# Letting the loads of batches 4 to 7 go one tile sooner

## The chip, the cores and the metric

The kernel runs on one core of a Trainium2 chip. The metric is the device time of one execution in microseconds (us). A profile covers one further execution, and its span (from the first to the last instruction) is about 1.8 us shorter than the time of the same execution.

Engines: PE is the tensor engine, DVE the vector engine, ACT the scalar engine, POOL is GpSimd and SP is SyncE. SP and POOL issue almost all DMAs here. "SPq" and "POOLq" are their queues.

## The reference, cut to what matters

```python
# q, k, v: (8 batches, 8 heads, 576 positions, 64)
kv  = np.einsum('bhsd,bhse->bhde', k, v)
out = np.einsum('bhsd,bhde->bhse', q, kv)
rms = np.sqrt(np.mean(out * out, axis=-1, keepdims=True) + 1e-06)
x   = (out / rms * g_norm)          # then reordered to (8, 576, 512)
xn  = (x - mean(x)) / np.sqrt(var(x) + 1e-06) * g_ln
y   = x + np.maximum(xn @ w_ch1, 0.0) @ w_ch2     # 512 -> 2048 -> 512
```

The 8 x 576 rows make 36 tiles of 128 rows, and four tiles make a block: blocks 0 to 8. Block 5 is tiles 20 to 23.

## The kernel before: the parts that matter

Before it emits anything, the kernel runs a small scheduler over all its steps, with guessed costs. That plan fixes the order of the instructions on each engine. What the chip then does is wait for semaphores in that order.

For batches 3 to 7, k and q are loaded by POOL straight into the layout in which they are used; q is then transposed by one large DMA on SP's queue (`q_turn_dma`, giving qT). Each tile's normalised rows xc are transposed by a smaller DMA on the same SP queue (`t_turn_dma`, giving xT). The first matmul of a block (L598) needs the xT of all its four tiles.

```python
def t_turn_dma(n):                                   # L544
    m, i = divmod(n, 4)
    nc.sync.dma_start_transpose(
        blk[m]["xT"][:, :, i * 128:(i + 1) * 128], st[n]["xc"])

def q_turn_dma(b):                                   # L421
    att[b]["qT"] = work.tile([128, 20, 128], bf16, tag="qT", name="qT", bufs=3)
    nc.sync.dma_start_transpose(
        att[b]["qT"], qp[b % 2].rearrange("p t h d -> p (t h d)"))
```

The loads don't go as soon as their buffer is free. POOL first runs a "gate": a copy of a single element out of the xT of an earlier tile, so that POOL, which runs in order, waits until that transpose has landed. With f the first tile of batch b (18, 22, 27 and 31 for batches 4 to 7), k, q and v wait for tiles f-7, f-6 and f-5:

```python
f = FIRST[b]
def gate(n):
    if b >= 3:
        m, i = divmod(n, 4)
        pool_do(0.1, lambda: nc.gpsimd.tensor_copy(                       # L691
            mark, blk[m]["xT"][:, 0, i * 128:i * 128 + 1]), done[n]["xT"])
# ...
gate(f - 7 if b > 3 else 5)
gate_turn()                                          # L695: waits for the last batch's qT
# ... load k
def some_q():
    gate(f - 6 if b > 3 else 6)
    # ... load q
def some_v():
    gate(f - 5 if b > 3 else 7)
    # ... load v
# ...
turn = add_dma("SP", ok - 12, qperm + load["q", b] + ..., lambda: q_turn_dma(b), ...)
turn.lag = 5.0 if by_slot else 0.0                   # for the plan alone
```

## Time and profile before

| | kernel before |
|---|---|
| time, first three runs | 296.15 us median (296.14 to 296.57) |
| span of the profiled execution | 295.1 us |
| PE busy | 283.1 us |
| PE idle before an instruction, before 26 us | 2.3 + 4.3 + 0.7 + 0.4 us |
| PE idle before an instruction, after 26 us | 0.7 us, once |

The busy time of PE, from the first part of the page:

```profile
span 295.1 us, 5184 instructions
PE 283.1 (96%) x2061; PEld 161.1 (55%) x2061; DVE 165.8 (56%) x360; ACT 143.1 (49%) x288; POOL 66.0 (22%) x92
```

The waits of PE (who waited, for whom, us in total, how often, the longest):

```profile
PE kv_ps L429 <- DMA vb<-in_v_dram: 4.3, 1, 4.3
PE scale_ps L308 <- DMA scales<-in_moe_g_ln_dram: 2.3, 1, 2.3
PE mm_ps L598 <- DMA xT<-xc: 0.7, 1, 0.7
PE mm_ps L583 <- ACT xT L540: 0.7, 1, 0.7
PE mm_ps L583 <- DMA w<-in_moe_w_ch_dram: 0.4, 1, 0.4
```

Four of these five waits come before 26 us, during the first loads. The third line is the only one later on. The timeline of PE around it (start, length, what; in brackets the idle time before it) shows that it is the start of block 5:

```profile
173.13 2.11 PE L617 MATMUL mm_ps<-w,m 128*128 128x512 bf16 x9
175.94 0.81 PE L598 MATMUL mm_ps<-xT,w 128*128 128x512 bf16 x3 [0.69 <-DMA xT<-xc]
```

What led to it stands in the timeline of the two issuing engines, from 153 us on. L261 is the load of q of batch 6, L233 the load of its v, L421 its qT, L544 an xT:

```profile
154.68 2.01 POOL L261 DMA_DIRECT2D qp<-in_q_dram  x1 [0.43 <-issue]
156.56 1.19 SPq L544 DMA_TRANSPOSE xT<-xc  x1
164.06 0.19 POOL L691 COPY mark<-xT 128x1 bf16<-128x1 bf16 x1 [6.68 <-DMA xT<-xc]
164.26 3.16 SPq L421 DMA_TRANSPOSE qT<-qp  x1
164.66 0.89 POOL L233 DMA_DIRECT2D vb<-in_v_dram  x1 [0.42 <-issue]
...
167.51 1.68 SPq L544 DMA_TRANSPOSE xT<-xc  x1
```

The transpose of tile 22 went at 156.56. The next in the queue was qT of batch 6, which had to wait for q; it went at 164.26. Tile 23, whose xc DVE had finished at 163.63, went at 167.51. The same instruction, looked at alone (its transfer, issue to landing):

```profile
L544 SPq DMA_TRANSPOSE xT<-xc x1: 1683/1683/1683, 167.5 to 167.5; - x1
...
DMA to landing us min/median/max: 8.1/8.1/8.1
```

So tile 23 stood 3.9 us in the queue and then flew 8.15 us, while the median xT flies 3.7 us. It landed at 175.66.

### The profile page before, as it was taken

To read this page: it belongs to the slowest core of one execution; us is meant where nothing else is said; L and a number is where in the kernel's file an instruction comes from. 1 tells how busy PE (TensorE), PEld (TensorE's weight loads), DVE (VectorE), ACT (ScalarE), POOL (GpSimd) and SP (SyncE) were. 2 spreads that over 40 slices of the span, in tenths; PEclk is the share of its full clock that TensorE was granted. 3 is DMA by queue.
4 is the path that set the end of the run, shared out by engine and by line. 5 is a ranking of instruction groups with operands and counts; after the bars stand their busy time and mean duration, and the time that the engine had idled before them with its cause. 6 is when DMAs were issued, how large, how long until landed. Compare 5 with 4: busy or idle time off the path is not lost.

```text
span 295.1 us, 5184 instructions
## 1 busy us (share of the span) xinstructions
PE 283.1 (96%) x2061; PEld 161.1 (55%) x2061; DVE 165.8 (56%) x360; ACT 143.1 (49%) x288; POOL 66.0 (22%) x92
## 2 busy tenths in 40 slices
PE   3799999999999999999999999999999999999995
PEld 1789955877745445444544445544454444444444
DVE  1397038759876886557655773577557755420022
ACT  3178972986857612671267117621762177006500
POOL 8882230208207024320403207020000000000000
PEclk9999999999999999999999999999999999999999
DMA  6999999749999998998399799999201310210012
GB/s 91 176 196 206 203 199 192 181 89 106 188 176 82 139 120 200 161 120 168 93 131 86 107 185 130 137 134 178 56 18 53 91 53 18 56 71 35 0 73 72
DMA packets 107388, 35.21 MB, mean 119 GB/s; under 512 B 85603, under 2 KB 103395, under 8 KB 107364
## 3 DMA queue, kind: packets, MB, share of 16 engines
q0 software_dynamic: 72608, 18.35, 65.2%
q1 hardware_dynamic: 34516, 16.39, 23.5%
q8 instruction: 16, 0.26, 0.4%
q10 hardware_dynamic: 240, 0.13, 0.2%
q14 instruction: 8, 0.07, 0.1%
HBM read 36.70 MB, written 9.44 MB: 156 GB/s over the span
## 4 chain that ended last, share of the span: by engine, by line
PE 87%; DMA 10%; POOL 1%; issue 1%; DVE 1%; ACT 0%; ACTq 0%; POOLq 0%
PE mm_ps L617 39%; PE mm_ps L598 33%; PE mm_ps L583 8%; DMA w<-in_moe_w_ch_dram 4%; DMA xT<-xc 3%; PE kv_ps L429 3%; PE out_ps L452 3%; DMA kb<-in_k_dram 3%; PE xT_ps L533 1%; PE qT_ps L401 0%; POOL qp L254 0%; POOL kb L233 0%; POOL w L334 0%; DVE ss L474 0%; POOL vb L233 0%
## 5 line engine op out<-in xcount | busy, mean ns | idle before, releaser
L617 PE MATMUL mm_ps<-w,m 128*128 128x512 bf16 (+2 forms) x608 | 130.3, 368 | 0.0
L598 PE MATMUL mm_ps<-xT,w 128*128 128x512 bf16 x448 | 100.8, 379 | 0.7 <-DMA xT<-xc 0.7
L605 ACT ACTIVATE m<-mm_ps 128x512 bf16<-128x512 f32 x112 | 66.8, 597 | 51.2 <-PE mm_ps L598 50.2
L617 PEld LDWEIGHTS <-m 128*128 128x128 bf16 x608 | 57.0, 98 | 59.7
L598 PEld LDWEIGHTS <-w 128*128 128x128 bf16 x448 | 43.0, 98 | 49.5 <-issue 1.2
L624 DVE SCALAR_TENSOR_TENSOR x<-mm_ps,rstd,x 128x512 f32<-128x512 f32 (+2 forms) x38 | 27.3, 721 | 41.9 <-PE mm_ps L617 41.8
L474 DVE TENSOR_REDUCE ss<-sq 128x8 f32<-128x512 f32 (+1 forms) x37 | 24.8, 670 | 46.0 <-ACT sq L465 45.9
L465 ACT ACTIVATE sq<-out_ps 128x512 f32<-128x512 f32 (+1 forms) x37 | 21.5, 584 | 52.3 <-PE out_ps L452 52.3
L583 PE MATMUL mm_ps<-xT,w 128*128 128x128 bf16 x512 | 30.9, 219 | 1.0 <-ACT xT L540 0.7
L583 PEld LDWEIGHTS <-w 128*128 128x128 bf16 x512 | 29.3, 98 | 2.1 <-issue 0.8
L526 DVE SCALAR_TENSOR_TENSOR xc<-x,mv,gl 128x512 bf16<-128x512 f32 (+1 forms) x37 | 27.1, 737 | 1.4 <-DVE mv L521 0.3
L469 DVE TENSOR_TENSOR xg<-out_ps,gn 128x512 f32<-128x512 f32 (+1 forms) x37 | 24.8, 669 | 0.3
L691 POOL COPY mark<-xT 128x1 bf16<-128x1 bf16 x15 | 5.1, 340 | 80.4 <-DMA xT<-xc 67.8
L590 ACT ACTIVATE m<-mm_ps 128x512 bf16<-128x512 f32 x32 | 18.3, 597 | 3.2 <-PE mm_ps L583 2.5
L504 DVE TENSOR_TENSOR x<-xg,inv 128x512 f32<-128x512 f32 x24 | 16.6, 693 | 0.8
L520 DVE BATCH_NORM_STATS2 stats<-x 128x6 f32<-128x512 f32 x24 | 16.6, 690 | 0.5
L444 DVE CAST kv_pack<-kv_ps 64x256 bf16<-64x256 f32 (+1 forms) x18 | 7.1, 392 | 15.8 <-PE kv_ps L429 15.7
L478 ACT ACTIVATE rms<-ss,eps_attn 128x8 f32<-128x8 f32 (+1 forms) x37 | 11.0, 298 | 9.9 <-DVE ss L474 9.9
L429 PE MATMUL kv_ps<-vb,kp 128*128 128x128 bf16 (+1 forms) x144 | 11.5, 231 | 4.3 <-DMA vb<-in_v_dram 4.3
L452 PEld LDWEIGHTS <-qT 128*128 128x128 bf16 x160 | 11.6, 98 | 7.3 <-DVE kv_pack L444 0.3
L452 PE MATMUL out_ps<-kv_pack,qT 128*128 128x128 bf16 x160 | 14.9, 220 | 0.1
L429 PEld LDWEIGHTS <-kp 128*128 128x128 bf16 (+1 forms) x168 | 10.9, 103 | 5.6 <-issue 2.6
(61 smaller groups left out, 171.4 us busy)
## 6 DMA issues: line engine op xcount, KB each, us to landing
out_dram<-x SPq DMA_DIRECT2D x28, 256.0 KB, 2.8
w<-in_moe_w_ch_dram POOLq DMA_DIRECT2D x8, 512.0 KB, 12.5
vb<-in_v_dram POOLq DMA_DIRECT2D x6, 512.0 KB, 9.1
kp<-in_k_dram POOLq DMA_DIRECT2D x5, 512.0 KB, 8.2
qp<-in_q_dram POOLq DMA_DIRECT2D x5, 512.0 KB, 9.5
out_dram<-x SPq DMA_DIRECT2D x14, 128.0 KB, 2.5
qb<-in_q_dram POOLq DMA_DIRECT2D x2, 512.0 KB, 15.7
qp<-in_q_dram POOLq DMA_DIRECT2D x10, 64.0 KB, 8.4
```

Source lines behind the costliest of these rows:

```text
L429: nc.tensor.matmul(ps[:, hp, :], lhsT=kp[b % 2][p, t, 2 * hp:2 * hp + 2, :].rearrange("p h d -> p (h d)"), rhs=(v5[b % 2][:, 2 * hp:2 * hp ...
L452: nc.tensor.matmul(o3[:, hp, :], lhsT=att[b]["qT"][:, 4 * t + hp, :], rhs=kv_pack[b % 3][:, hp, :], start=(i == 0), stop=(i == len(bs) - 1))
L465: nc.scalar.activation(sq[:, h0:h1, :], st[n]["ps", h0][:, h0:h1, :], func=AF.Square)
L469: nc.vector.tensor_mul(xg[:, h0:h1, :], st[n]["ps", h0][:, h0:h1, :], gn.to_broadcast([128, h1 - h0, D]))
L474: nc.vector.tensor_reduce(ss[:, h0:h1, :], st[n]["sq"][:, h0:h1, :], axis=AX.X, op=ALU.add)
L526: nc.vector.scalar_tensor_tensor(xc[:, f0:f1], in0=st[n]["x"][:, f0:f1], scalar=blk[m]["mv"][:, i, 0:1], in1=gl[:, f0:f1], op0=ALU.subtrac ...
L583: nc.tensor.matmul(ps[:, d, :], lhsT=w1[c][:, kk, d * 128:(d + 1) * 128], rhs=blk[m]["xT"][:, kk, i * 128:(i + 1) * 128], start=(kk == 0), ...
L590: nc.scalar.activation(st[n]["m1"][:, c, :, :], st[n]["m1ps", c], func=AF.Relu)
L598: nc.tensor.matmul(ps, lhsT=w1[c][:, kk, d * 128:(d + 1) * 128], rhs=blk[m]["xT"][:, kk, :], start=(kk == 0), stop=(kk == nKm - 1))
L605: nc.scalar.activation(blk[m]["m1", c][:, d, :], blk[m]["m1ps", g], func=AF.Relu)
L617: nc.tensor.matmul(st[n]["m2ps", f0], lhsT=m1_piece(n, c, d), rhs=w2[c][:, d, f0:f1], start=(c == 0 and d == 0), stop=(c == 3 and d == 3))
L624: nc.vector.scalar_tensor_tensor(x[:, f0:f1], in0=st[n]["m2ps", f0], scalar=blk[m]["rstd"][:, i, :], in1=x[:, f0:f1], op0=ALU.mult, op1=AL ...
```

## The change

The intent is to let each of these loads go one tile sooner, so that it lands earlier and what waits for it has more room.

```diff
-            gate(f - 7 if b > 3 else 5)
+            gate(f - 8 if b > 3 else 5)
             gate_turn()
@@ some_q @@
-                gate(f - 6 if b > 3 else 6)
+                gate(f - 7 if b > 3 else 6)
@@ some_v @@
-                gate(f - 5 if b > 3 else 7)
+                gate(f - 6 if b > 3 else 7)
```

The number of instructions doesn't change (the traces below count 5184 and 5183; now and then a record is missing from a trace). On PE, DVE, ACT and POOL their order is the same as before. On SP, the plan moves qT of batch 6 ahead of tile 22, and qT of batch 7 ahead of tile 26.

## The prediction

> **What bounds the kernel.** The tensor engine. The page gives PE 283.1 of 295.1 us busy, granted clock 1.00 throughout. Summing the idle times before PE instructions in the list of waits: 2.3 + 4.3 + 0.7 + 0.4 us, all before 26 us, during the first loads; after that one wait is left, of 0.7 us at 175.9 us, on L598 (first matmul of block 5, tiles 20 to 23), for the DMA transpose xT<-xc of tile 23. The change touches nothing before 85 us, so 0.7 us (0.24% of the time) is all that it can win; it could lose more.
>
> **What it does.** It adds and removes no instruction. The twelve one-element copies on GpSimd that hold back the loads of k, q and v for batches 4 to 7 wait for the transposed tile before the one they waited for. The instruction orders: PE, DVE, ACT and POOL the same; on SP the qT transposes of batches 6 and 7 move ahead of one xT transpose (tiles 22 and 26).
>
> **Where loads can move**, from the timeline (issue; landing):
> - Batch 4: k is held until the previous qT lands (89.15), so k (89.95) and q (92.43) stay; v goes from 103.4 to about 95.5.
> - Batch 5: k (114.7) and q (117.6) stay, held by qT at 113.93; v goes from 127.1 to about 120.
> - Batch 6: k 144.5 to about 140; q 154.7 to about 149.5; v 164.7 to about 158.
> - Batch 7: k 179 to about 169; q 181.4 to about 178; v 193 to about 185.
>
> **The one wait.** xc of tile 23 was ready at 163.63, but the SP queue stood at the qT transpose of batch 6, which waited for q (landed 163.92 and 164.11). So tile 23 was issued at 167.51, and landed at 175.66, 8.1 us later against a median of 3.7, beside that qT transpose (landed 174.99) and v (174.63). The Trainium skill, "DMA: Bandwidth & Descriptors", section "Issuing engines are not separate DMA queues", says that DMAs of all issuers run on the same 16 engines and interleave; the trace agrees: xT takes 2.4 us alone, 8.1 us beside both. After the change q of batch 6 lands at about 159, qT is issued then, tile 23 at about 163.7, landing at 167 to 171, before PE wants it at 175.2. The wait goes.
>
> **What it costs.** k, q and v follow each other more closely, so xT transposes of tiles 13, 14, 17, 21, 22 and 25 share the engines more and land up to about 6 us later; tiles 22 and 26 also stand behind qT in the queue (22: about 156.6 to 162; 26: 187 to 191). What counts is the last tile of each block: tile 15 had 4.9 us to spare (landed 110.96, wanted 115.8), tile 19 6.1 us, tile 27 2.9 us (202.84 against 205.8). I expect 15 and 19 to keep over 2 us and tile 27 to gain, as v and qT of batch 7 are earlier. DVE and ACT are half idle and don't set the pace.
>
> **Time.** 296.15 - 0.7 = 295.5 us; range 295.1 to 296.3. Faster by over 2%: 0.005; within 2%: 0.985; slower by over 2%: 0.01.
>
> **What would show it.** Right: span about 294.4; no PE wait after 30 us; tile 23 issued near 163.7; v of batch 4 issued near 95.5; PE busy time unchanged. Wrong: a PE wait at 115.8, 145.4, 175.2 or 205 us on xT; or tile 23 still behind qT because q of batch 6 landed no earlier.
>
> **What would make it wrong.** Crowded loads delaying tile 15, 19, 23 or 27 by more than its slack: each us beyond it costs one us. Or run-to-run scatter of the first loads (296.14 to 296.57 before), as large as the effect.

## The result, and the profile after

Ratios are computed as the mean time of one kernel's fast runs over the mean time of the other's fast runs of the same rounds, so they are not quite the ratio of the medians quoted.

| | before | after |
|---|---|---|
| time, six runs each | 296.16 us median (294.80 to 296.57) | 295.35 us median (295.18 to 295.76) |
| ratio | | 0.998, 95% interval 0.9959 to 1.0 |
| span of the profiled execution | 295.06 us | 293.96 us |
| start of block 2 | 85.72 | 85.33 |
| block 4 start to block 5 start | 30.49 | 29.64 |
| tile 23: xc ready, issued, landed | 163.63, 167.51, 175.66 | 163.24, 163.67, 166.17 |
| block 5 starts | 175.94 | 174.69 |

The page and the waits of PE after:

```profile
span 294.0 us, 5183 instructions
PE 283.4 (96%) x2061; PEld 161.6 (55%) x2061; DVE 166.1 (57%) x360; ACT 143.3 (49%) x288; POOL 65.5 (22%) x92
```

```profile
PE kv_ps L429 <- DMA vb<-in_v_dram: 3.1, 1, 3.1
PE scale_ps L308 <- DMA scales<-in_moe_g_ln_dram: 2.2, 1, 2.2
PE qT_ps L401 <- DMA qp<-in_q_dram: 0.8, 1, 0.8
PE mm_ps L583 <- ACT xT L540: 0.7, 1, 0.7
```

The wait on xT is gone, and the other waits are still those of the first 26 us. The timeline of PE at the start of block 5 (no idle time in brackets any more), of the issuing engines before it, and tile 23 alone:

```profile
174.69 2.11 PE L598 MATMUL mm_ps<-xT,w 128*128 128x512 bf16 x9
```

```profile
147.79 2.01 POOL L261 DMA_DIRECT2D qp<-in_q_dram  x1 [0.42 <-issue]
...
154.39 0.89 POOL L233 DMA_DIRECT2D vb<-in_v_dram  x1
...
156.30 5.07 SPq L421 DMA_TRANSPOSE qT<-qp  x1
161.46 3.43 SPq L544 DMA_TRANSPOSE xT<-xc  x2
```

```profile
L544 SPq DMA_TRANSPOSE xT<-xc x1: 1219/1219/1219, 163.7 to 163.7; - x1
...
DMA to landing us min/median/max: 2.5/2.5/2.5
```

q of batch 6 is issued 6.9 us sooner and v 10.3 us sooner. qT goes at 156.30, ahead of tile 22. Tile 23 is issued 0.43 us after its xc is ready and flies 2.5 us, because v had landed at 160.56 and the next load (k of batch 7) went only at 167.19. It lands 8.5 us before PE asks for it.

Where did the 1.10 us of span go? All but one of the stretches between the starts of blocks 2 to 8 are the same to 0.01 us in both traces. Block 4 to block 5 gives 0.85 us. The start of block 2 gives 0.39 us, before any changed load is issued. The stretch from the start of block 8 to the end is 0.15 us longer after (31.48 against 31.33), for which no cause was looked for. The 0.69 us of idle time on PE thus stands for 0.85 us of time: the stretch is the better measure of what this wait costs, since the idle time is taken from modelled ends of matmuls.

### The profile page after: what moved, and what is told of

The parts are those of the page before. It is cut to its first block, busy times and chain, and to the rows that moved or that the text cites. A ratio compares the mean times of both kernels' runs of the same rounds, so it can differ in the third digit from the quotient of the medians.

```text
span 294.0 us, 5183 instructions
## 1 busy us (share of the span) xinstructions
PE 283.4 (96%) x2061; PEld 161.6 (55%) x2061; DVE 166.1 (57%) x360; ACT 143.3 (49%) x288; POOL 65.5 (22%) x92
## 2 busy tenths in 40 slices
DMA packets 107388, 35.21 MB, mean 120 GB/s; under 512 B 85603, under 2 KB 103395, under 8 KB 107364
## 4 chain that ended last, share of the span: by engine, by line
PE 90%; DMA 7%; POOL 1%; issue 1%; DVE 0%; POOLq 0%
PE mm_ps L617 42%; PE mm_ps L598 33%; PE mm_ps L583 8%; DMA w<-in_moe_w_ch_dram 5%; PE kv_ps L429 3%; PE out_ps L452 3%; DMA vb<-in_v_dram 3%; PE xT_ps L533 1%; POOL kb L233 1%; PE qT_ps L401 0%; POOL vb L233 0%; DVE x L624 0%; POOL qp L254 0%; POOLq L943 0%
## 5 line engine op out<-in xcount | busy, mean ns | idle before, releaser
L691 POOL COPY mark<-xT 128x1 bf16<-128x1 bf16 x15 | 6.3, 423 | 64.2 <-DMA xT<-xc 55.4
```

## The experiments

**Theories.** The main theory was that of the prediction: the gain is the one wait for tile 23, and it goes because q of batch 6 lands sooner, so that tile 23 doesn't stand behind qT. Rivals: (A) the loads of every batch have a share; (B) the difference is scatter of the first loads; (C) the changed order on SP gives the gain, not the earlier loads; (D) and (E) only the sharing of the DMA engines, or only the standing in the queue, matters.

The first four ran together on one chip, beside 11 runs of the kernel before (295.58 us median, 294.99 to 297.0).

### Batch 6 alone

```diff
-gate(f - 7 if b > 3 else 5)
+gate(f - (8 if b == 6 else 7) if b > 3 else 5)
```

and the same for q and v.

> Only batch 6's three loads are let go one tile sooner; batches 4, 5 and 7 as before. Main theory (the gain is the one PE wait of 0.7 us for tile 23, which batch 6's q and v loads caused): no PE wait after 30 us, block 4 to block 5 start 29.6 us as in the changed kernel (30.5 before), time about 295.4, ratio 0.997 to 0.998. Rival A (every batch's loads contribute a share): a wait of 0.3 to 0.5 us is left. Rival B (the difference is scatter of the first loads): PE wait at block 5 may go, but the time does not follow it.

Measured: 295.07 us median (294.78 to 295.75), ratio 0.9983 (0.9964 to 1.0003). Block 4 to 5 took 29.64 us, with no PE wait there; tile 23 was issued at 163.43 and landed at 167.47. Batch 6 alone does what the whole change does; rival A is not needed.

### All batches but batch 6

```diff
-gate(f - 7 if b > 3 else 5)
+gate(f - (7 if b == 6 else 8) if b > 3 else 5)
```

and the same for q and v.

> Batches 4, 5 and 7 are let go one tile sooner, batch 6 as before; all instruction orders as before. Main theory: the wait of about 0.7 us at block 5 stays (0.4 to 1.2), time about 296.15, ratio 1.000. Rival A (each batch has a share): wait smaller, time about 295.6. Rival B (scatter): cannot be told from the other runs by time.

Measured: 295.12 us median (294.74 to 298.17), ratio 0.9997 (0.9963 to 1.0032). PE did wait at block 5, but less than expected: 0.16 us idle, and 29.96 us from block 4 to 5, which is 0.32 us over 29.64.

```profile
174.65 2.10 PE L598 MATMUL mm_ps<-xT,w 128*128 128x512 bf16 x9 [0.16 <-issue]
```

The trace names no releaser for this short wait ("issue"), but PE starts 0.25 us after tile 23 lands (174.40), as in the kernel before (0.28 us). Tile 23 stood 3.7 us (162.88 to 166.62) and flew 7.8 us, beside qT and v as in the kernel before. A smaller wait is also what rival A foretold; but batch 6 alone took the whole wait away, and the last group shows that its size changes by itself from one execution to the next. So the wait belongs to batch 6, and its size is not fixed. This raised a doubt about the 0.7 us of the prediction.

### The order on SP alone

The gates are those of the kernel before. A negative lag makes the plan put qT where the changed kernel has it.

```diff
-turn.lag = 5.0 if by_slot else 0.0
+turn.lag = (-2.0 if b >= 6 else 5.0) if by_slot else 0.0
```

> The gates of the kernel before, with the SP order of the changed one (qT of batch 6 ahead of tile 22, of batch 7 ahead of tile 26), got by the plan's lag alone. Main theory (what helps is that q lands sooner, not the order): q lands near 164 as before, so tiles 22 and 23 both stand behind qT, tile 23 is issued at 168.5 to 170 and lands at 175.5 to 178: PE wait at block 5 of 0.7 to 2.5 us, time 296.1 to 298. Rival C (the order is what gives the gain): no wait, time 295.4.

Measured: 295.25 us median (294.77 to 295.61), ratio 0.9982 (0.9962 to 1.0003), block 4 to 5 29.64 us: no wait. The expectation of the main theory was wrong. The timeline of the issuing engines, and tile 23 alone:

```profile
162.83 3.08 SPq L421 DMA_TRANSPOSE qT<-qp  x1
166.00 2.53 SPq L544 DMA_TRANSPOSE xT<-xc  x2
168.59 0.19 POOL L691 COPY mark<-xT 128x1 bf16<-128x1 bf16 x1 [11.12 <-DMA xT<-xc]
...
169.19 0.89 POOL L233 DMA_DIRECT2D vb<-in_v_dram  x1 [0.42 <-issue]
```

```profile
L544 SPq DMA_TRANSPOSE xT<-xc x1: 1218/1218/1218, 167.3 to 167.3; - x1
...
DMA to landing us min/median/max: 2.4/2.4/2.4
```

q landed only at 162.68, and tiles 22 and 23 both stood behind qT; tile 23 was issued at 167.32, as late as before. But v is gated by tile 22, which now stood too. So v went at 169.19 instead of 164.66, and tile 23 flew in 2.45 us instead of 8.15. Standing for 4.1 us in the queue is not enough to make the wait.

### The changed loads with the old order on SP

```diff
 # in the changed kernel
-turn.lag = 5.0 if by_slot else 0.0
+turn.lag = (7.0 if b >= 6 else 5.0) if by_slot else 0.0
```

> The gates of the changed kernel, with the SP order of the kernel before. Main theory: q of batch 6 lands near 156, tile 22 is issued at about 156.2, qT right after it, tile 23 at about 163.7 without standing; no PE wait after 30 us, time 295.4. Rival C (the order gives the gain): the wait of 0.7 us is back, time 296.1.

Measured: 294.79 us median (294.70 to 295.05), ratio 0.9972 (0.9954 to 0.9989), block 4 to 5 29.64 us, tile 23 issued at 162.40, landed at 164.83. The gain doesn't need the new order either, so rival C falls as the only cause. This is the one ratio whose interval lies wholly under 1. Its profile shows nothing after the start of block 2 that the changed kernel lacks (208.47 us from there to the end, against 208.48 us in the second profile of the changed kernel); its block 2 started early, at 84.46. It was not run beside the changed kernel, and is not claimed to beat it.

The next four ran together on another chip, beside 7 runs of the kernel before (295.61 us median, 294.91 to 297.58).

### qT of batch 6 behind tile 23

Loads as before; a longer lag in the plan moves qT of batch 6 behind tile 23 and one store.

```diff
-turn.lag = 5.0 if by_slot else 0.0
+turn.lag = (8.0 if b == 6 else 5.0) if by_slot else 0.0
```

> Loads as before; only the qT transpose of batch 6 moves behind tile 23 in the SP queue (and behind one store). Tests whether standing in the queue is enough of a cause by itself. Main theory: tile 23 is issued at 163.7 instead of 167.5, shares the engines with v alone for most of its flight, lands at 168 to 173, no PE wait; qT of batch 6 is issued near 167 and lands by 176, which tile 26 and 27 bear; time about 295.4. Rival D (only the sharing with v matters, not the standing): tile 23 still lands near 174.6 when v does; wait under 0.3 us or none, but landing after 173.5.

Measured: 295.62 us median (295.21 to 295.9), ratio 0.9992 (0.9954 to 1.003), block 4 to 5 29.64 us. Tile 23 was issued at 163.26, ahead of v (164.98) and qT (165.59), and landed at 165.96. Taking the standing away is enough; but it also let tile 23 fly before qT and before the packets of v, so the run does not tell the two apart.

### Only the gate of q, only the gate of v

```diff
# first kernel: q alone
-gate(f - 6 if b > 3 else 6)
+gate(f - (7 if b == 6 else 6) if b > 3 else 6)
# second kernel: v alone
-gate(f - 5 if b > 3 else 7)
+gate(f - (6 if b == 6 else 5) if b > 3 else 7)
```

> Only the q gate of batch 6 is one tile sooner. Main theory: q follows k, is issued near 147 and lands near 156.5, so qT goes at about 158 and tile 23 does not stand; tile 22 flies with less beside it, lands near 160, and so v goes sooner by itself (about 160 instead of 164.7). No PE wait after 30 us.

> Only the v gate of batch 6 is one tile sooner (v then follows q at once, near 157). Main theory: q is slowed by sharing with v and lands at 164 to 168; qT and so tile 23 are issued no sooner than before (tile 23 at 167.5 to 171), but v has landed by then (165 to 170) and tile 23 lands at 170 to 174.5: no wait or under 0.3 us. Rival E (standing in the queue is the whole cause, sharing does nothing): tile 23 flies 8 us as before, wait of 0.7 us or more.

One look each, 295.13 and 295.02 us, and 29.64 us from block 4 to 5 in both. With q alone, tile 23 didn't stand (162.79 to 162.82) but shared its flight with v (158.81 to 167.15) and with the end of qT (157.75 to 166.97), and flew 5.3 us. With v alone, it stood 4.8 us behind qT (162.64 to 167.46), but v had landed at 166.32, and it flew 2.5 us. Removing either half of the delay is enough: rivals D and E, each half as the whole cause, fall together.

### One tile later

```diff
-gate(f - 7 if b > 3 else 5)
+gate(f - 6 if b > 3 else 5)
```

and f-5 for q, f-4 for v.

> The change the other way: batches 4 to 7 let go one tile later than in the kernel before (the plan then moves instructions on PE, DVE and SP too, so this is no pure test). Main theory: waits for the last tile of a block or for qT, kv appear at more than one block, total PE wait after 30 us 2 to 10 us, time 297 to 306. Rival (loads have slack and one tile is nothing): within 0.5 us of before.

Measured: 295.36 us median (295.02 to 295.57), ratio 0.9985 (0.994 to 1.0031); no PE wait after 26 us. The expectation was wrong by far. The plan reacted: it put qT of batch 6 behind tile 23 by itself, so tile 23 was issued at once (162.80), and landed at 169.54: it flew 6.7 us beside the load of q (161.28 to 170.46), so it isn't v alone that makes a flight long. The order on PE and DVE changed too, so this run is no pure test. The loads have more room than the main theory gave them. "Sooner" was not what the kernel needed.

The last four ran together on a third chip, beside 11 runs of the kernel before (295.60 us median, 294.88 to 297.53).

### Both kernels again

> The kernel before, unchanged, against itself: how much of 0.2% is scatter, and whether its one late PE wait is there each time. Theory so far (tile 23 lands within a us of the time at which PE asks for it, so the wait is a matter of chance): block 4 to block 5 takes 29.64 us plus 0 to 1 us, all other stretches between block starts are the same to 0.02 us, the start of block 2 falls anywhere between 84.4 and 86 us. Ratio 1.000 with an interval of about 0.2% either way. Rival B (the whole difference between the kernels is scatter of the first loads): stretch of block 4 to 5 is 29.64 here too.

> The changed kernel a second time, beside the kernel before against itself on the same chip. Theory: block 4 to block 5 exactly 29.64 us, tile 23 lands 7 us or more ahead; ratio 0.997 to 0.9995. Rival B: ratio as likely over 1 as under it.

The kernel before against itself: 295.93 us median (294.91 to 297.06), ratio 1.0006 (0.9978 to 1.0035). The changed kernel: 295.19 us median (294.88 to 296.11), ratio 0.999 (0.9962 to 1.0019); in its trace block 4 to 5 took 29.64 us and tile 23 landed 9.0 us ahead, as expected. In the second trace of the kernel before, tile 23 stood 4.4 us and flew 6.5 us, and PE did not wait at block 5 at all:

```profile
L544 SPq DMA_TRANSPOSE xT<-xc x1: 1463/1463/1463, 167.0 to 167.0; - x1
...
DMA to landing us min/median/max: 6.5/6.5/6.5
```

```profile
174.01 2.75 PE L598 MATMUL mm_ps<-xT,w 128*128 128x512 bf16 x12
```

It landed at 173.52, half a microsecond before block 5 began at 174.01. So the wait that the change removes is there in some executions of the kernel before and not in others. A stretch of 29.64 us here is also what rival B foretold; the times are compared below.

### q and v of batch 6 one tile later, all orders kept

```diff
 def some_q():
-    gate(f - 6 if b > 3 else 6)
+    gate(f - (5 if b == 6 else 6) if b > 3 else 6)
-turn.lag = 5.0 if by_slot else 0.0
+turn.lag = ({6: -4.0, 7: 2.0}.get(b, 5.0)) if by_slot else 0.0
```

The lag keeps the order of every engine as in the kernel before.

> The dose the other way, with all five instruction orders those of the kernel before: q of batch 6 (and v behind it) let go one tile later. Theory (standing in the queue behind qT plus a flight beside qT and v adds up to the wait): q is issued near 159 and lands at 168 to 170, tile 23 is issued at 171 to 174 and lands at 175 to 180, PE wait at block 5 of 0.5 to 4 us, and the time is longer than the kernel before by 0.2 to 3.5 us. Rival (loads have slack and tile 23 was bad luck): wait under 0.7 us as before.

Measured: 295.22 us median (294.79 to 295.61), ratio 0.9984 (0.996 to 1.0009), block 4 to 5 29.64 us: no wait, against my expectation.

```profile
158.48 2.01 POOL L261 DMA_DIRECT2D qp<-in_q_dram  x1 [0.42 <-issue]
...
160.96 1.22 POOL L233 DMA_DIRECT2D vb<-in_v_dram  x1
...
166.90 3.52 SPq L421 DMA_TRANSPOSE qT<-qp  x1
170.51 1.22 SPq L544 DMA_TRANSPOSE xT<-xc  x1
```

```profile
L544 SPq DMA_TRANSPOSE xT<-xc x1: 1220/1220/1220, 170.5 to 170.5; - x1
...
DMA to landing us min/median/max: 2.4/2.4/2.4
```

Tile 23 stood 8.1 us, twice as long as in the kernel before. But q and v passed their gates together, v followed q at once and landed at 168.88, before tile 23 was issued. The flight took 2.4 us, and the tile landed 0.9 us before block 5 began (173.89). A load that goes later made this wait go away too.

### Two tiles sooner

```diff
-gate(f - 7 if b > 3 else 5)
+gate(f - 9 if b > 3 else 5)
```

and f-8 for q, f-7 for v.

> All loads of batches 4 to 7 two tiles sooner than before. Theory (with no PE wait left after 30 us there is nothing more to win): block 4 to 5 29.64 us, ratio as that of the changed kernel within 0.1%; if loads crowd too much, a wait for the last tile of a block shows, under 1 us. Rival A (each tile sooner gains): another 0.5 us less.

Measured: 295.21 us median (294.83 to 296.22), ratio 0.9987 (0.9961 to 1.0013), block 4 to 5 29.64 us, no PE wait after 26 us. No further gain, and no new wait.

### What the runs say together

In every trace, PE asks for tile 23 at the same distance after its xc is ready: 11.45 us, which is the start of block 4 plus 29.64 us, less the end of xc (in the kernel before 145.44 + 29.64 - 163.63). About 0.27 us of that is spent between landing and the first matmul (175.66 to 175.94, and 174.40 to 174.65 in the other trace that waits). PE waits where standing plus flight exceeds about 11.2 us.

| run | stood | flew | sum | load in flight beside it | block 4 to 5 |
|---|---|---|---|---|---|
| kernel before | 3.88 | 8.15 | 12.03 | v, from 164.66 | 30.49 |
| all but batch 6 | 3.74 | 7.78 | 11.52 | v, from 163.76 | 29.96 |
| kernel before, again | 4.40 | 6.55 | 10.95 | v, from 163.54 | 29.64 |
| q and v later | 8.07 | 2.44 | 10.51 | none, v had landed | 29.64 |
| v alone | 4.82 | 2.52 | 7.34 | none, v had landed | 29.64 |
| one tile later | 0.03 | 6.74 | 6.77 | q, from 161.28 | 29.64 |
| order alone | 4.12 | 2.44 | 6.56 | none, v issued only at 169.19 | 29.64 |
| two tiles sooner | 0.03 | 5.59 | 5.62 | k of batch 7, from 160.98 | 29.64 |
| q alone | 0.03 | 5.28 | 5.31 | v, from 158.81 | 29.64 |
| batch 6 alone | 0.03 | 4.05 | 4.07 | v, from 156.33 | 29.64 |
| changed kernel | 0.43 | 2.50 | 2.93 | none, v had landed | 29.64 |

(qT behind tile 23, the old order on SP with the changed loads, and the second trace of the changed kernel have sums of 2.4 to 2.7 us.) In these runs only standing behind qT together with a flight beside the load of v comes near the room or exceeds it, but for "q and v later", where 8.07 us of standing alone left 0.9 us. Where the two come together, the sum lies so near the limit (10.95 to 12.03 us against 11.2) that one execution waits and the next doesn't.

A rival is left in the table: in all three runs at its top, qT is also still in flight ahead of tile 23, and tile 23 lands 0.7 to 0.9 us after it. Does qT make the flight long, or v? The packets of the kernel before tell. qT moves as 2,560 packets of 256 bytes and tile 23 as 512. From 164.3 to 169.5 us, SP's queue (q1) moved 2,449 packets, so qT was nearly done. Then the packets of v came (on q0, POOL's queue), and from 169.5 to 172.0 us there were:

```profile
q0 software_dynamic: 753, 0.39, 149.6%
q1 hardware_dynamic: 105, 0.03, 8.0%
```

SP's queue nearly stopped while v moved, and qT's last packets and tile 23 were held up together; in the run of q alone it moved 4 packets from 163.0 to 165.5 us, against 805. So v makes the flight long, of qT and of tile 23 alike. The two delays are not quite separate, though: what tile 23 stands behind is held up by the same load.

As for the time: the kernel before (41 runs) and the kernel with batch 6 left as before (6 runs) went over 296.25 us in 9 of 47 runs, up to 298.17; the changed kernel and all other variants in none of 52 (highest 296.22). The threshold was chosen after seeing the numbers, and those long runs have no trace. That they are larger waits of the same kind fits, but is not shown. A fairer count of the same runs is the mean in each of the four sets of rounds (the result's and the three groups'), with all changed kernels whose traces show no late wait taken together (fast runs alone, 50 in all): they lie under the kernel before in all four, by 0.60, 0.59, 0.43 and 0.46 us, together by an estimated 0.52 us (0.31 to 0.74, 95% interval, by resampling the runs within the sets). So rival B, scatter alone, does not explain the times of these kernels together. For the changed kernel alone it isn't excluded: the upper ends of its two intervals are 1.0 and 1.0019.

## Why the prediction was right, and where it was off

- **The class and the range** held: 295.35 us against 295.5 (295.1 to 296.3), within 2%. That the number came so near is partly luck: of the 1.10 us by which the two profiled spans differ, 0.39 us lies in the first loads, and the second trace of the kernel before has no wait to win.
- **What bounds the kernel, and that only one wait was to be won:** right for the traced execution. PE busy time stayed at about 283 us, and after the change PE waits for nothing after 26 us.
- **The moves of the loads** came within about 4 us: for batch 6, predicted 140, 149.5 and 158 for k, q and v, measured 137.1, 147.8 and 154.4; for v of batch 7, predicted 185, measured 180.6. Tile 22 was issued at 161.5 (predicted 162), tile 23 at 163.67 (163.7), tile 26 at 190.4 (191).
- **The size was the weak term.** "0.7 us (0.24% of the time) is all that it can win" took one execution's wait as a property of the kernel. Three traces with batch 6 as before show 0.85, 0.32 and 0.00 us over 29.64. Their mean, 0.39 us, is an estimate of the usual gain; the mean times of the last group differ by 0.36 us (295.70 for the 11 runs beside it to 295.34). The warning in the prediction that scatter is as large as the effect was right: block 2 starts anywhere from 84.46 to 85.97 us in the 14 traces, and the kernel before against itself has an interval of about 0.3% either way.
- **The cause was told too narrowly.** "Tile 23 still behind qT because q of batch 6 landed no earlier" was named as a sign of failure. In the run of the order alone, tile 23 was behind qT, q had landed less than 2 us sooner (162.68 against 164.11), and there was no wait. Standing for 4 us needs a crowded flight as its partner; the prediction had both parts (the late issue at 167.51 and the flight of 8.1 us) but built its sign of failure on the first.
- **The cost ran the other way where it mattered.** Tiles 15 and 19 were expected to lose slack and keep over 2 us. They gained: from 4.9 to 7.4 us and from 6.1 to 9.0 us (landed 108.06, wanted 115.41; landed 136.09, wanted 145.05), because the load of v was over sooner. Tile 15 had flown beside it (v landed at 109.90, now at 105.56); tile 19 had stood behind the qT of batch 5, which had flown beside its v (landed at 134.15, now at 129.42). Tile 27 gained as predicted, from 2.9 to 9.0 us. It was a middle tile that paid: tile 14 landed at 107.54 instead of 102.91. The gate of k of batch 5 now waits for it, but the next gate, for qT, held that load until 112.85 anyway, and PE did not wait.

Open: the long runs of the kernel before, and why the part after block 8 took 0.15 us more in one trace of the changed kernel but not in the other (31.48 and 31.33 us).

## What to carry to other kernels

A small DMA that the busiest engine waits for was delayed here in two places: behind its neighbour in its queue, and on the engines that it shares with bulk loads; add both and compare the sum with the room from "data ready" to "data wanted". A load can be moved sooner, or later, or another queue order chosen: all of them worked here, because each pulled the two delays apart. And a wait of 0.7 us in one profile is one sample: take a second profile of the unchanged kernel before putting a price on it.

## What the Trainium skill lacked or had wrong

Nothing that was used of it proved wrong; these points it lacks.

- "DMA: Bandwidth & Descriptors", section "Issuing engines are not separate DMA queues", says that DMAs of all issuers interleave on the same 16 engines; the runs agree, but the page gives no price for a small transpose beside a bulk load. Here tile 23's transpose of 128 x 512 bf16 landed 2.4 to 2.7 us after issue with no load's packets beside it, and 4.05 to 8.15 us after it beside a 512 KB load issued by GpSimd (in the longest three, and in the 5.28 us of q alone, with the end of a qT ahead of it). Nor were the shares even: in 2.5 us, 105 packets of SP's queue against 753 of GpSimd's.
- The same page, section "Rules for kernel authors", says "A transpose next to ordinary DMAs needs nothing". That concerns correctness, and all runs were correct; the page doesn't add that it can cost time, as the same 2.4 against 8.15 us show.
- The same page, section "Bandwidth", gives 6.15 us of DMA time for a load of 1 MB issued by GpSimd. The loads of k, q and v read 1 MB of f32 each and write 512 KB of bf16, and took a median of 8.2, 9.5 and 9.1 us from issue to landing. These are not the same measure, and most packets here are small (85,603 of 107,388 are under 512 B); the page has no line for a load that casts and scatters like these.
- No page says how much a DMA's landing varies from one execution to the next. Tile 23's transpose took 8.15 and 6.55 us in two traces of the kernel before, and 7.78 us in the same instruction orders with only other batches' loads moved.
